# A two-stage convolution and joint network with its gradients: the rows of ge by small transfers and a shuffle, the last chunk on 128 partitions, and some squares allowed on GpSimd

## The chip, the cores and the metric

The kernel runs on one core of one Trainium2 chip. The metric is device time in microseconds (us) of that core. A core has five engines that run their own instruction streams in order: TensorE (PE; its weight loads are PEld), VectorE (DVE), ScalarE (ACT), GpSimd (POOL) and SyncE (SP, which here only issues DMAs). They wait for one another by semaphores. The kernel before was timed in three runs, and one further execution was profiled.

## The reference: what is computed

```python
# B, T, D, K, U = 2, 16000, 256, 3, 8;  T1 = T/2, T2 = T/4
h  = gelu(conv3(x, w1))[:, ::2]            # (B, 8000, 256)
f  = gelu(conv3(h, w2))[:, ::2]            # (B, 4000, 256)
fe = f @ w_f                               # (B, 4000, 256)
ge = g @ w_g                               # (B, 8, 256)
j  = tanh(fe[:, :, None] + ge[:, None])    # (B, 4000, 8, 256)
out = j @ w_o                              # (B, 4000, 8, 256)
# and, for a given grad_out of out's shape, the gradients of x, w1, w2, g, w_f, w_g and w_o
```

The bulk of the work hangs on `j`, which has eight rows (u) for each of the 8000 positions. For each u the kernel computes the tanh, `out`, the product of grad_out with w_o transposed, its product with j squared minus one (whose sums over positions and over u give the gradients of ge and fe), and w_o's gradient, which is j's rows times grad_out.

## The kernel before

**Tiling.** The 8000 positions of both sequences are cut into 17 chunks: one of 256, fifteen of 512 and a last one of 64. A chunk lies in blocks of up to 128 positions (`A` blocks of `Pw`). Chunk 8 holds the end of sequence 0 and the start of sequence 1. Channels lie on the 128 partitions in two halves (kt, mt); this is the transposed layout. Matmuls that sum over positions, as w_o's gradient does, need the other layout, positions on partitions, which the code calls rows.

**Stages.** `stage_a` does both convolutions of a chunk and FE, the projection fe. `stage_j` does everything with eight u, in four pairs (`pair`). `stage_de` goes back through the convolutions and adds up the weight gradients of the chunk. `gg_out` ends with the gradients of g, w_g and w_o. While chunk k is in `stage_j`, chunk k+1 is in `stage_a` and chunk k-1 in `stage_de`.

**One pair of u** (line 634 on): ACT computes JT, the tanh with ge as its bias (L644). JR, the same tanh in rows, comes in one of two ways. In chunks 0 and 1 (`TRANS`) PE transposes JT (L663) and ACT or DVE moves the result out of PSUM. In the other chunks DVE adds FER (fe in rows, made in `stage_a`) and GEB (ge's eight rows, the same on each partition; L668) and ACT takes the tanh (L673). PE adds JR times GO, the loaded grad_out, to the sum GWO; GWO stays in PSUM for the whole kernel. GOT is GO transposed by a DMA. PE multiplies it by w_o transposed (WOT), DVE multiplies the result by JSQ minus one (L716, with the sum over positions as a second output), and the results of the eight u are added up in ZS by DVE (L733), the last into NGFE (L730). JSQ is JT squared, by ACT (L703) or DVE (L705). PE computes JT times w_o in four blocks, ACT or DVE moves them to OUT_SB (L345, L350), and SP stores them.

**GEB** (`make_geb`, line 602): PE multiplies w_g by one column of ge's input repeated over 128 columns, so that the result stands on each partition: 16 matmuls of 256 columns and four moves of 512 out of PSUM. It is made three times: for sequence 0, for sequence 1 and, as GEBX, for chunk 8, where POOL first fills GM with the columns of both (L608).

**The last chunk** has 64 positions in one block, so its blocks of rows fill 64 partitions. Its GO is one load with all eight u, and its GOT one DMA transpose.

**What sets the order.** The code gives each operation an engine (or two that may take it), a cost, a due time and the buffers that it reads and writes. `Flow.issue` (line 107) plays all of it through on these costs before anything runs, and writes the instruction streams in the order in which operations start there. A small edit thus moves operations in every stream. Buffers come from classes with a few slots (`jsq` has 2, `go`, `got` and `out` have 3, `ps`, the PSUM banks, has 7), and an operation that opens a buffer waits until a slot is free. The choice of ACT or DVE for a move, too, is made there.

Most matmuls carry line 336 in the profile (the helper `mm`), moves out of PSUM lines 345 to 352 (`evac`), DMAs lines 360 and 362.

Of the kernel before, what the change touches and what calls it, by code (L numbers as in the profile page):

```python
# [12 lines left out]
ALU = mybir.AluOpType  # L13
# [207 lines left out]
def kernel(  # L221
# [99 lines left out]
    W2T = fixed([P, KT, KK * D], BF16, "W2T")  # L321
    W1T = fixed([P, KT, KK * D], BF16, "W1T")
    GR8 = fixed([U, B, D], BF16, "GR8")
    ACC1 = fixed([P, KK, KT, D], FP32, "ACC1")
# [95 lines left out]
    def load_go(k, up, at, after=()):  # L420
        c = chunks[k]
        A, Pw = c.A, c.Pw
        GO = buf("go", [P, NB, 2, V], BF16, "GO")
        if c.last:

            dma("SP", lambda: GO[:Pw].rearrange("p a u v -> p (a u v)"),
                lambda: bass.AP(tensor=go_.tensor, offset=go_.offset + c.c0 * U * V, ap=[[U * V, Pw], [1, U * V]]),
                r=[], w=[GO], bytes_=Pw * U * V * 2, new=[GO], at=at, after=after)
            st[k]["GO"] = {up: GO for up in range(UP)}
            return  # L430
        dma("SP", lambda: GO[:Pw, 0:A].rearrange("p a u v -> p a (u v)"),
            lambda: bass.AP(tensor=go_.tensor, offset=go_.offset + (c.c0 * U + 2 * up) * V,
                            ap=[[A * U * V, Pw], [U * V, A], [1, 2 * V]]),
            r=[], w=[GO], bytes_=Pw * A * 1024, new=[GO], at=at, after=after, sub="go")
        st[k].setdefault("GO", {})[up] = GO

    def load_got(k, up, at):
        c = chunks[k]
        A, Pw = c.A, c.Pw
        GO = st[k]["GO"][up]  # L440
        GOT = buf("got", [P, NB, 2, KT, P], BF16, "GOT")
        if c.last:
            dma("SP", lambda: GOT[:, :, :, :, :Pw].rearrange("p a u k c -> p (a u k) c"),
                lambda: GO[:Pw].rearrange("p a u v -> p (a u v)"), r=[GO], w=[GOT],
                bytes_=Pw * U * V * 2, new=[GOT], transpose=True, at=at)
            st[k]["GOT"] = {up: GOT for up in range(UP)}
            return
        dma("SP", lambda: GOT[:, 0:A, :, :, :Pw].rearrange("p a u k c -> p (a u k) c"),
            lambda: GO[:Pw, 0:A].rearrange("p a u v -> p (a u v)"), r=[GO], w=[GOT],
            bytes_=Pw * A * 1024, new=[GOT], transpose=True, at=at, sub="got")  # L450
        st[k].setdefault("GOT", {})[up] = GOT
# [86 lines left out]
    def stage_a(k, t0, dt):  # L538
# [45 lines left out]
        for mt in range(KT):  # L584
# [6 lines left out]
            evac(lambda mt=mt: FE[:, 0:A, mt, :Pw], lambda ps=ps: fl(ps[:, :W], A), W, r=[ps], w=[(FE, mt)])  # L591
        if k not in TRANS:
            S["FER"] = rows(k, "fer", "FER", FE, 0, A, [(FE, 0), (FE, 1)], pe=Pw, lag=0.0 if c.first else 500.0)
# [4 lines left out]

    n_gwo = sum(len(c.blk) for c in chunks) * U * KT
    gwo_cnt = [0]  # L600

    def make_geb(kind):
        GEB = buf("gx" if kind == "x" else "geb", [P, U, D], BF16, "GEB")
        if kind == "x":
            px = [c.px for c in chunks if c.px is not None][0]
            GM = buf("out", [P, KT, U, P], BF16, "GM")
            for b, lo, hi in ((0, 0, px), (1, px, P)):
                op("POOL", 1200.0, lambda e, b=b, lo=lo, hi=hi: nc.gpsimd.tensor_copy(  # L608
                    out=GM[:, :, :, lo:hi], in_=gT[b][:].unsqueeze(3).to_broadcast([P, KT, U, hi - lo])),
                   r=[gT[b]], w=[(GM, b)], new=[GM] if b == 0 else [])  # L610
            rd = [GM]
        else:
            rd = [gT[kind]]
        for u2 in range(UP):
            ps = psum()

            def mms(e, u2=u2, ps=ps):
                for j in range(2):
                    u = 2 * u2 + j
                    for kt in range(KT):  # L620
                        lhsT = GM[:, kt, u, :] if kind == "x" else gT[kind][:, kt, u:u + 1].to_broadcast([P, P])
                        mm(ps[:, j * D:(j + 1) * D], lhsT, WG[:, kt, :], kt == 0, kt == KT - 1)
            op("PE", c_pe([D] * 4), mms, r=rd + [WG], w=[ps], new=[ps] + ([GEB] if u2 == 0 else []))
            evac(lambda u2=u2: GEB[:, 2 * u2:2 * u2 + 2].rearrange("p u d -> p (u d)"), lambda ps=ps: ps[:], 512,
                 r=[ps], w=[(GEB, u2)])
        return GEB

    def stage_j(k, t0, dt, GEB):
# [3 lines left out]
        FE = S["FE"]  # L632

        def pair(up):
            F.now = tu = t0 + dt * up / UP
            q = dt / UP
            JT = buf("jt", [P, 2, KT, CW], BF16, "JT")
            GOT, GO = S["GOT"].pop(up), S["GO"].pop(up)
            u0 = up if c.last else 0
            for j in range(2):  # L640
                for mt in range(KT):
                    def jt(e, j=j, mt=mt):
                        for b, lo, hi, _ in c.segs:
                            nc.scalar.activation(  # L644
                                out=fl(JT[:, j, mt, :W], A)[:, :, lo:hi], in_=FE[:, 0:A, mt, lo:hi], func=ACT.Tanh,
                                bias=GE[:, b, mt, 2 * up + j:2 * up + j + 1], scale=1.0)
                    op("ACT", sum(c_act((s[2] - s[1]) * A, ptr=True) for s in c.segs), jt,
                       r=[(FE, mt)] + [(GE, s[0]) for s in c.segs], w=[(JT, (j, mt))],
                       new=[JT] if j == 0 and mt == 0 else [], at=tu - q * (1.0 - (2 * j + mt) / 4), sub="jt")
            halves = [c.blk[h:h + 2] for h in range(0, A, 2)]  # L650
            for h, tbs in enumerate(halves):
                JR = buf("jr", [P, 2, 2, D], BF16, "JR")
                th = tu + q * (h / 2 - 0.5)
                n, lo, m = len(tbs), tbs[0][0], Pw
                if k in TRANS:
                    tr = psum(BF16)
# [19 lines left out]
                def gwo(e, tbs=tbs, JR=JR):  # L676
                    for tb, m in tbs:
                        for j in range(2):
                            for d2 in range(KT):
                                n = gwo_cnt[0]  # L680
                                mm(GWO[:, d2, :], JR[:m, tb % 2, j, d2 * P:(d2 + 1) * P], GO[:m, up if c.last else tb, j, :],
                                   n == 0, n == n_gwo - 1)
                                gwo_cnt[0] = n + 1
                op("PE", c_pe([V] * (4 * n)), gwo, r=[JR, GO], w=[], at=tu + q * (h / 2 + 0.3), sub="gwo")
            OUT = buf("out", [P, NB, 2, V], BF16, "OUT_SB")
            for step in range(4):
# [5 lines left out]
                def gj(e, j=j, d2=d2, ps=ps):  # L692
                    for kt in range(KT):
                        mm(fl(ps[:, :W], A), WOT[:, kt, d2 * P:(d2 + 1) * P], GOT[:, u0:u0 + A, j, kt, :Pw], kt == 0, kt == KT - 1)
                if u and d2 == 0:
                    NGZ = buf("ngz", [P, KT, CW], FP32, "NGZ")
                op("PE", c_pe([W] * KT), gj, r=[GOT, WOT], w=[ps], new=[ps, NGZ] if u and d2 == 0 else [ps])
                if d2 == 0:
                    JSQ = buf("jsq", [P, KT, CW], BF16, "JSQ")

                    def jsq(e, j=j, JSQ=JSQ):
                        if e == "ACT":
                            nc.scalar.activation(out=JSQ[:, :, :W], in_=JT[:, j, :, :W], func=ACT.Square)  # L703
                        else:
                            nc.vector.tensor_tensor(out=JSQ[:, :, :W], in0=JT[:, j, :, :W], in1=JT[:, j, :, :W], op=ALU.mult)  # L705
                    op(("ACT", "DVE"), (c_act(KT * W), c_dve(KT * W, 0.5)), jsq, r=[(JT, (j, 0)), (JT, (j, 1))], w=[JSQ],
                       new=[JSQ], at=F.now - q / 4, sub="jsq")
# [28 lines left out]
                for tb, m in c.blk:  # L736
                    if tb != step:
                        continue
                    ps = psum()

                    def out_mm(e, tb=tb, m=m, ps=ps):
                        for jj in range(2):
                            for kt in range(KT):
# [4 lines left out]
                         r=[ps], w=[(OUT, tb)])  # L748
            F.now = tu + q
            dma("SP", lambda: bass.AP(tensor=o_.tensor, offset=o_.offset + (c.c0 * U + 2 * up) * V,  # L750
                                      ap=[[A * U * V, Pw], [U * V, A], [1, 2 * V]]),
# [24 lines left out]
    def stage_de(k, t0, dt):  # L776
# [136 lines left out]
        for bl, m in c.sblk:  # L913
# [21 lines left out]
            if bl % 2 == 1 or bl == A - 1:  # L935
# [4 lines left out]
                def put(p0, p1, lo, hi, GX=GX, row=row):  # L940
                    dma("SP", lambda: row_ap(gx_, row + 4 * A * p0 + lo, 4 * A, p1 - p0, hi - lo),
                        lambda: GX[p0:p1].rearrange("p a c d -> p (a c d)")[:, lo * D:hi * D], r=[GX], w=[],
# [123 lines left out]
    make_ge()  # L1066
    GEB = make_geb(0)
    GEBX = None
    for k in range(NG + 1):
# [15 lines left out]
        if k + 1 < NG and chunks[k + 1].px is not None:  # L1085
            F.now = t0 + Wk * 0.3
            GEBX = make_geb("x")
        if k < NG:
            F.stage = "j" + part(k)
            stage_j(k, t0, Wk, GEBX if c.px is not None else GEB)  # L1090
        if k < NG and c.px is not None:
            F.now = t0 + Wk * 0.3
            GEB = make_geb(1)
        if k + 1 < NG:
# [42 lines left out]
```

## Time and profile before

| what | us |
|---|---|
| three timed runs | 794.16, 795.49 (median), 795.92 |
| the profiled execution: its time | 793.3 |
| the profiled execution: first to last instruction (span) | 791.0 |
| PE busy in the span | 773.1 (98%) |
| ACT busy | 727.0 (92%) |
| DVE busy | 716.1 (91%) |
| POOL busy | 83.8 (11%) |

The granted TensorE clock was 0.998 over the span. Busy times of PE count a matmul from its start to its modelled end, and neighbours overlap, so two things tell more than the share: the gaps between matmuls, and the spacing of their starts. All four streams can be read as a timeline, as busy time in windows, and as a chain of waits that is followed back from the last instruction.

### The profile page before, as it was taken

The numbers are of one execution on the slowest core, as the hardware profiler recorded it, in microseconds if no ns is written. First come the engines' busy times: TensorE is split into PE (matmuls) and PEld (weight loads), VectorE is DVE, ScalarE is ACT, GpSimd is POOL, SyncE is SP. The second block draws the span as 40 slices with busy tenths as digits, with TensorE's granted clock in tenths as the row PEclk, the third lists the DMA queues.
The fourth block names the chain that finished last, engine by engine and source line by source line (L and its number), as shares of the span: only waits on it lengthen the run. The fifth ranks groups of instructions, "written<-read, shape, count | busy, mean of one in ns | idle before, by whom it ended". The sixth has DMA issues, their size and how long they took to land.

```text
span 791.0 us, 15682 instructions
## 1 busy us (share of the span) xinstructions
PE 773.1 (98%) x5687; PEld 537.9 (68%) x5722; DVE 716.1 (91%) x1514; ACT 727.0 (92%) x1176; POOL 83.8 (11%) x227
## 2 busy tenths in 40 slices
PE   8989999999999999999999999999999999999996
PEld 6657577576675767767677675776767767577764
DVE  5899999897998989999999898989989899899874
ACT  6999999999999998999999998999999999898752
POOL 2110010201002011110101102010020110102010
PEclk9999999999999999999999999999999999999999
DMA  9999999999999899999999999998999999999874
GB/s 208 205 190 202 214 263 229 244 228 281 202 231 256 231 238 195 229 267 219 233 218 254 228 217 233 214 264 209 230 235 214 239 237 228 237 264 255 201 177 123
DMA packets 381809, 178.82 MB, mean 226 GB/s; under 512 B 307586, under 2 KB 375460, under 8 KB 379812
## 3 DMA queue, kind: packets, MB, share of 16 engines
q1 hardware_dynamic: 380516, 177.03, 99.8%
q8 instruction: 45, 0.74, 0.4%
q10 hardware_dynamic: 1056, 0.52, 0.2%
q14 instruction: 32, 0.26, 0.1%
q0 software_dynamic: 160, 0.27, 0.1%
HBM read 51.42 MB, written 50.34 MB: 129 GB/s over the span
## 4 chain that ended last, share of the span: by engine, by line
PE 72%; ACT 11%; DVE 9%; DMA 3%; issue 3%; SPq 1%; POOL 0%; DVEq 0%; ACTq 0%
PE ps L336 60%; PE GWO L336 10%; ACT JT L644 2%; DVE g_s L516 2%; ACT JSQ L703 2%; DMA GOT<-GO 2%; ACT g_sq L510 2%; PE psb L489 2%; DVE NGZ L716 1%; ACT OUT_SB L345 1%; ACT JR L673 1%; DVE g_sq L529 1%; SPq L360 1%; ACT HTo L513 1%; DMA XC<-in_x_dram 1%
## 5 line engine op out<-in xcount | busy, mean ns | idle before, releaser
L644 ACT ACTIVATE JT<-FE,GE 128x512 bf16<-128x512 bf16 (+4 forms) x288 | 180.7, 680 | 0.0
L716 DVE SCALAR_TENSOR_TENSOR NGZ<-JSQ,ps 128x512 f32<-128x512 bf16 (+3 forms) x252 | 149.7, 607 | 2.5 <-PE ps L336 2.0
L336 PE MATMUL ps<-WO,JT 128*128 128x256 bf16 (+1 forms) x1008 | 148.2, 273 | 1.3 <-DVE NGZ L716 1.3
L336 PE MATMUL ps<-GOT,WOT 128*128 128x512 bf16 (+2 forms) x544 | 146.5, 362 | 1.8 <-DMA GOT<-GO 1.6
L345 ACT CAST OUT_SB<-ps 128x512 bf16<-128x512 f32 (+1 forms) x210 | 123.0, 600 | 17.4 <-PE ps L336 17.3
L703 ACT ACTIVATE JSQ<-JT 128x1024 bf16<-128x1024 bf16 (+2 forms) x128 | 128.6, 1005 | 9.2 <-DVE NGZ L716 8.2
L336 PEld LDWEIGHTS <-JT 128*128 128x128 bf16 (+1 forms) x1008 | 98.2, 98 | 54.9 <-issue 2.0
L336 PE MATMUL GWO<-GO,JR 128*128 128x256 bf16 (+1 forms) x1008 | 130.8, 273 | 0.1
L673 ACT ACTIVATE JR<-JR 128x1024 bf16<-128x1024 bf16 (+1 forms) x116 | 121.6, 1054 | 4.1 <-DVE JR L668 3.8
L733 DVE TENSOR_TENSOR ZS<-ZS,NGZ 128x1024 f32<-128x1024 f32 (+2 forms) x102 | 115.1, 1128 | 0.3
L336 PEld LDWEIGHTS <-JR 128*128 128x128 bf16 (+1 forms) x1008 | 98.2, 98 | 17.8 <-issue 1.3
L516 DVE SCALAR_TENSOR_TENSOR g_s<-g_sq,ps 128x512 bf16<-128x512 bf16 (+2 forms) x102 | 65.2, 639 | 41.0 <-ACT HTo L513 32.2
L336 PEld LDWEIGHTS <-W 128*128 128x128 bf16 x612 | 58.1, 98 | 59.5 <-issue 2.2
L336 PE MATMUL ps<-XC,W 128*128 128x512 bf16 (+2 forms) x408 | 84.3, 362 | 0.9 <-DMA XC<-in_x_dram 0.9
L668 DVE TENSOR_TENSOR JR<-FER,GEB 128x1024 bf16<-128x1024 bf16 (+1 forms) x116 | 79.2, 684 | 2.2 <-PE GWO L336 1.0
L336 PEld LDWEIGHTS <-X 128*128 128x128 bf16 (+1 forms) x756 | 73.8, 98 | 9.4
L772 DVE TENSOR_TENSOR ACC<-ACC,ps 128x512 f32<-128x512 f32 x90 | 59.4, 678 | 16.9 <-PE ps L336 16.7
L336 PEld LDWEIGHTS <-WOT 128*128 128x128 bf16 x544 | 51.6, 98 | 23.9 <-DMA GOT<-GO 1.8
L347 ACT ACTIVATE GX_SB<-ps 128x512 bf16<-128x512 f32 (+1 forms) x109 | 64.1, 615 | 1.6 <-PE ps L336 1.1
L510 ACT ACTIVATE g_sq<-ps 128x512 bf16<-128x512 f32 (+2 forms) x102 | 59.1, 580 | 3.4 <-PE ps L336 2.7
L525 ACT ACTIVATE g_s<-g_s 128x1024 bf16<-128x1024 bf16 (+2 forms) x51 | 52.1, 1025 | 6.3 <-DVE g_s L516 6.1
L336 PE MATMUL ps<-GHoR,X 128*128 128x256 bf16 (+1 forms) x378 | 57.7, 273 | 0.0
(139 smaller groups left out, 1113.6 us busy)
## 6 DMA issues: line engine op xcount, KB each, us to landing
GO<-in_grad_out_dram SPq DMA_DIRECT2D x60, 512.0 KB, 5.3
out_dram<-OUT_SB SPq DMA_DIRECT2D x60, 512.0 KB, 5.3
X<-in_x_dram SPq DMA_DIRECT2D x15, 1088.0 KB, 8.3
out_dram<-GX_SB SPq DMA_DIRECT2D x30, 512.0 KB, 5.5
GO<-in_grad_out_dram SPq DMA_DIRECT2D x5, 256.0 KB, 5.4
GOT<-GO SPq DMA_TRANSPOSE x65, 5.0
out_dram<-OUT_SB SPq DMA_DIRECT2D x4, 256.0 KB, 3.5
XC<-in_x_dram SPq DMA_TRANSPOSE x62, 5.5
```

The lines of the kernel that those rows point to most:

```text
L336: nc.tensor.matmul(ps_ap, lhsT=lhsT, rhs=rhs, start=start, stop=stop)
L345: nc.scalar.copy(out=dst(), in_=src())
L347: nc.scalar.activation(out=dst(), in_=src(), func=ACT.Copy, scale=scale)
L510: op("ACT", c_act(W, True), lambda e, mt=mt, ps=ps: nc.scalar.activation(out=sq[:, 0:A, mt, :Pw], in_=fl(ps[:, :W], A), func=ACT.Square, s ...
L516: op("DVE", c_dve(W), lambda e, mt=mt, ps=ps: nc.vector.scalar_tensor_tensor(out=s[:, 0:A, mt, :Pw], in0=sq[:, 0:A, mt, :Pw], scalar=1.0, ...
L644: nc.scalar.activation(out=fl(JT[:, j, mt, :W], A)[:, :, lo:hi], in_=FE[:, 0:A, mt, lo:hi], func=ACT.Tanh, bias=GE[:, b, mt, 2 * up + j:2 ...
L668: op("DVE", c_dve(n * 2 * D, 0.5), lambda e, lo=lo, n=n, m=m, JR=JR: nc.vector.tensor_tensor(out=JR[:m, 0:n], in0=S["FER"][:m, lo:lo + n]. ...
L673: op("ACT", c_act(n * 2 * D), lambda e, n=n, m=m, JR=JR: nc.scalar.activation(out=JR[:m, 0:n], in_=JR[:m, 0:n], func=ACT.Tanh), r=[JR], w= ...
L703: nc.scalar.activation(out=JSQ[:, :, :W], in_=JT[:, j, :, :W], func=ACT.Square)
L716: nc.vector.scalar_tensor_tensor(out=fl(zap(), A)[:, :, lo:hi], in0=fl(JSQ[:, d2, :W], A)[:, :, lo:hi], scalar=1.0, in1=fl(ps[:, :W], A)[: ...
L733: nc.vector.tensor_tensor(out=a, in0=a, in1=b, op=ALU.add)
L772: op("DVE", c_dve(512), lambda e: nc.vector.tensor_tensor(out=acc_ap().rearrange("p k d -> p (k d)"), in0=acc_ap().rearrange("p k d -> p ( ...
```

## The change

Four edits:

1. **GEB.** PE computes ge's rows once for each sequence, 8 partitions by 256, and they are moved to a small tile GER. GEB is set to zero on POOL; four DMAs of 4 KB from POOL's queue write all eight rows into partitions 0, 32, 64 and 96; a VectorE shuffle copies the first partition of each group of 32 to the whole group. GEB of the second sequence is made the same way. GEBX is put together by two DVE copies out of both.
2. **The last chunk.** Two u stand side by side: the odd u of a pair on partitions 64 to 127. GO comes by two loads, GOT by a transpose of 128 partitions, JR by PE transposes of JT, and w_o's gradient and `out` by half as many matmuls. Its four stores of `out` become two, after the last pair. FER of that chunk is not made.
3. **Squares.** In chunks 0 and 1 an operation JSQ may also go to POOL, as a product.
4. **Stores.** The last chunk's stores of x's gradient are issued by ACT and no longer by SP.

The core of the diff:

```diff
+    def make_geb(b):
+        GEB = buf("geb", [P, U, D], BF16, "GEB")
+        op("POOL", 2100.0, lambda e: nc.gpsimd.memset(GEB[:], 0.0), r=[(GER, b)], w=[GEB], new=[GEB])
+        for q in range(0, P, 32):
+            dma("POOL", lambda q=q: GEB[q:q + 1], lambda: GER[:, b, :], r=[(GER, b)], w=[(GEB, q)], bytes_=4096)
+        def spread(e):
+            v = GEB[:].rearrange("p u d -> p (u d)").bitcast(FP32)
+            nc.vector.stream_shuffle(v, v, [0] * 32)
+        op("DVE", 66.0 + c_dve(U * D // 2), spread, r=[GEB], w=[GEB], sub="geb", lag=45000.0 if b == 0 else 100000.0)
+        return GEB
+    def mix_geb(G0, G1):
+        px = [c.px for c in chunks if c.px is not None][0]
+        GEB = buf("gx", [P, U, D], BF16, "GEB")
+        op("DVE", c_dve(U * D, 0.25), lambda e: nc.vector.tensor_copy(out=GEB[:], in_=G1[:]), r=[G1], w=[GEB], new=[GEB])
+        op("DVE", c_dve(U * D, 0.25), lambda e: nc.vector.tensor_copy(out=GEB[:px], in_=G0[:px]), r=[G0], w=[GEB])
+        return GEB
+    def ge_rows():
+        for b in range(B):
+            ps = psum()
+            def mms(e, b=b, ps=ps):
+                for kt in range(KT):
+                    mm(ps[:U, 0:D], gT[b][:, kt, :], WG[:, kt, :], kt == 0, kt == KT - 1)
+            op("PE", c_pe([D] * KT), mms, r=[gT[b], WG], w=[ps], new=[ps])
+            evac(lambda b=b: GER[:, b], lambda ps=ps: ps[:U, 0:D], D, r=[ps], w=[(GER, b)])
...
+                if c.last:
+                    tr = psum(BF16)
+                    def trs(e, tr=tr):
+                        for kt in range(KT):
+                            nc.tensor.transpose(out=tr[:2 * Pw, kt * P:(kt + 1) * P], in_=JT[:, 0, kt, :2 * Pw], identity=ident[:])
...
-                        for j in range(2):
+                        for j in range(1 if c.last else 2):
...
                     def jsq(e, j=j, JSQ=JSQ):
+                        if e == "POOL":
+                            nc.gpsimd.tensor_tensor(out=JSQ[:, :, :W], in0=jtw(JT, j), in1=jtw(JT, j), op=ALU.mult)
...
-                    op(("ACT", "DVE"), (c_act(KT * W), c_dve(KT * W, 0.5)), jsq, r=[(JT, (j, 0)), (JT, (j, 1))], w=[JSQ],
+                    pool = k < 2
+                    op(("ACT", "DVE", "POOL") if pool else ("ACT", "DVE"),
+                       (c_act(KT * W), c_dve(KT * W, 0.5)) + ((100.0 + 2.0 * KT * W,) if pool else ()), jsq, r=[(JT, (j, 0)), (JT, (j, 1))], w=[JSQ],
...
-                    dma("SP", lambda: row_ap(gx_, row + 4 * A * p0 + lo, 4 * A, p1 - p0, hi - lo),
+                    dma("ACT" if c.last else "SP", lambda: row_ap(gx_, row + 4 * A * p0 + lo, 4 * A, p1 - p0, hi - lo),
...
-    GEB = make_geb(0)
-    GEBX = None
+    GEB = GEBX = None
...
         if k + 1 < NG and chunks[k + 1].px is not None:
             F.now = t0 + Wk * 0.3
-            GEBX = make_geb("x")
+            GEB1 = make_geb(1)
+            GEBX = mix_geb(GEB, GEB1)
+        if k == 1:
+            F.now = t0 + Wk * 0.1
+            ge_rows()
+            GEB = make_geb(0)
```

## The prediction, made before the changed kernel had run

> **What bounds the kernel now.** I read the page's first part and the head of the chain of waits first:
>
> ```profile
> PE 773.1 (98%) x5687; PEld 537.9 (68%) x5722; DVE 716.1 (91%) x1514; ACT 727.0 (92%) x1176; POOL 83.8 (11%) x227
> ...
> PE 72%; ACT 11%; DVE 9%; DMA 3%; issue 3%; SPq 1%; POOL 0%; DVEq 0%; ACTq 0%
> ```
>
> Three engines are above 90%, so shares settle little. Busy time in windows of 20 us tells where PE has air (columns: stretch, its length, then busy us and instructions of PE, PEld, DVE, ACT, POOL, then clock, DMA share, GB/s):
>
> ```profile
> 0.00:20.00 20.00, 16.55 (x140) 13.13 (x141) 11.98 (x40) 13.10 (x32) 4.79 (x17) 1.00 0.96 207
> 20.00:40.00 20.00, 19.62 (x149) 13.00 (x148) 17.95 (x45) 19.63 (x36) 2.08 (x7) 1.00 1.15 207
> 40.00:60.00 20.00, 17.30 (x129) 11.33 (x128) 18.41 (x49) 20.00 (x33) 3.66 (x11) 1.00 1.04 187
> 60.00:80.00 20.00, 19.95 (x174) 15.25 (x173) 19.78 (x40) 19.82 (x33) 0.53 (x2) 1.00 1.02 210
> 80.00:100.00 20.00, 18.43 (x123) 11.34 (x122) 18.32 (x37) 18.84 (x30) 1.70 (x7) 1.00 0.94 216
> ...
> 460.00:480.00 20.00, 20.00 (x155) 14.87 (x153) 18.89 (x38) 18.95 (x28) 0.70 (x3) 1.00 1.00 225
> ...
> 760.00:780.00 20.00, 18.70 (x171) 14.10 (x170) 12.39 (x57) 7.60 (x18) 1.62 (x6) 1.00 0.68 175
> ```
>
> From 100 to 720 us PE is full: in the timeline its matmuls start 0.216 us (512 columns) or 0.109 us (256) apart, almost without a gap. There, PE work that goes is time that goes. Only the ramp (0 to 90) and the end leave PE waiting. The chain names what holds the ramp (start, length, what):
>
> ```profile
> 12.08 0.20 DVE g_s L533
> ...
> 14.05 0.89 ACT JT L644 x2
> 14.94 0.47 ACT GEB L345
> ...
> 28.88 0.70 DVE g_s L516
> ...
> 44.93 1.03 PE ps L336 x8
> ...
> 75.88 5.20 DMA GO<-in_grad_out_dram
> ...
> 81.15 8.07 DMA GOT<-GO
> ```
>
> ACT holds the time from 13.5 to 28.9, DVE from there to 44.9, PE to 76; then a load of GO and its transpose end late, and PE stands from 87.4 to 89.3.
>
> **The sum, against the profiled execution** (span 791.0, its time 793.3; the median of the timed runs is 795.49, so I add the change to that). Counts are from the order of the built changed program, which has no times.
>
> *PE work.* Out go 48 matmuls of GEB and GEBX (48 x 0.109 = 5.23 us) and, in the last chunk, 8 of GWO and 8 of `out` (1.74). In come four for GER (0.44) and six more transposes (six by 0.057, from L663's spacing, 0.34). Net 6.2 us less. By place: 3.05 in the ramp, as both GEB stand at 13.3 to 16.4 and 22.8; 1.74 for GEBX, near 340; 1.40 in the last chunk. The last two lie where PE is full: **-3.15**.
>
> *Ramp.* Less PE work does not help here; ACT and DVE set the pace. I follow the second chunk's NGFE, which DVE writes at 86.9 and PE takes at 90.1.
> - ACT from its first JT to the second chunk's HTo: the order has two GEB moves fewer (0.47 each, by their spacing), one JR move fewer (0.90), one square fewer (0.53) and one OUT_SB move more (0.47): **-1.9**. DVE loses 2.9 us before the first NGFE (its instructions there, each at the median spacing of its kind, add up to 31.4 and not 34.3), but waits for ACT in that stretch, so I give nothing for it. From the first NGFE to the second it is 39.3 and 39.2.
> - GEB's two memsets on POOL stand in the order right behind G1o's (11.75 us) with no wait. From rows of L368 (512 elements 0.52, 1280 elements 1.16 us) one takes 1.8 us. DVE's L533 at 12.08 is on the chain, and such copies and scalings do not pass a POOL instruction: at 728.11 an L531 took 0.26 instead of 0.19 us under a memset that ended at 728.32. So L533 ends some **+1.6** later (0 if it does pass).
> - The squares. Eight go to POOL: two of 512 elements (chunk 0) and six of 1024 (chunk 1). [...]
>
> ```profile
> 309.89 2.21 POOL L608 COPY GM<-gT 128x640 bf16<-128x640 bf16 x2 [9.21 <-DMA out_dram<-OUT_SB]
> ```
>
> ```profile
> 310.80 1.58 DVE L533 TENSOR_SCALAR g_s<-g_s 128x1024 bf16<-128x1024 bf16 x1
> ```
>
> This L533 usually takes 0.42; it ended only after the second copy (310.54, 1.56 us long). L668 with two SBUF operands took 0.86 at 240.27 instead of 0.68, against a POOL copy of 0.39. Instructions that read PSUM (L716, L350) never stretched. The price of a square: no row has a POOL product. POOL's copies (254 elements 0.39, 1408 elements 1.56) give about 1.2 us for 1024 elements of one operand and 2.3 for two read one after the other; I take 2.1, nearer the second, and half for 512. What DVE loses by it lies between nothing and all of it. In the order, an instruction that can be shut out is followed by one or two that read PSUM, 0.6 each, so some 1.3 pass beside a square: **0.8** lost for each large one, 0.3 for a small one. Ahead of the first NGFE stand the two small ones and one large: +1.4. Behind it stand five: 4.0, less the 2.4 us that DVE idles between both NGFE (41.75 us for 39.3 of work): **+1.6**.
> - The GOT wait at 87.4 lies behind these delays: **-1.7**.
>
> Sum of the ramp: -1.9 + 1.6 + 1.4 + 1.6 - 1.7 = **+1.0**.
>
> [...]
>
> *End.* In the order 10.7 us of PE work stand behind the last chunk's NGFE, where there were 5.5; PE's gap of 1.25 at 777.2, which waits for it, is filled: **-1.0**. SP's last two stores are a stage at 787.24, which landed at 789.67, and 1 x 768 of GX at 787.80. With GX on ACT, the stage moves up one issue (0.57) and is the last: **-0.7**.
>
> *At nothing.* The DMAs of GEB are issued by POOL at about 17 to 25 us, at 0.61 each like GR's, and the shuffle is needed at some 85, where L668 starts; without that cover all of DVE would stand behind it. Shuffle and GEBX's copies add some 2 x 1.15 (as L733's 1.2 for 1024 words; 0.4 as L527 at the least) and 2 x 0.65 us to DVE, which has more than 1 us of air in each window where PE is full, and loses seven GEB moves. The last chunk's two loads of GO and its transpose have some 6 us until PE reads GOT at 762.2; smaller rows of 512 B could eat that. ACT and DVE wait for PE from 746 on, so fewer moves there give nothing.
>
> Total: -3.15 + 1.0 - 1.7 = **-3.8**: span 787.2, this execution 789.5, and for the median **791.7**.
>
> **Rivals.**
> - *The squares are free* (chance 0.27). DVE reads PSUM while POOL works, and the memsets pass. For it: twenty L733 that overlapped POOL never stretched (at most 1.22 us); it was POOL that waited (G1o's copy at 154.13 took 1.33 us, not 0.39). Then the ramp gives -1.9 - 1.7, the total -8.5: **787.0**.
> - *The squares shut DVE out nearly whole* (0.16), the slower end. Each large one costs 1.8, each small one 0.6: 3.0 ahead of the first NGFE, 9.0 - 2.4 behind it; ramp -1.9 + 1.6 + 3.0 + 6.6 - 1.7 = +7.6, total +2.7: **798.2**. It decides from 1.4 us a large square on (0.8 + 3.8 / 6). For it: five large squares come in the 42 us where DVE idles 2.4; against it: POOL has to wait too. [...]
> - *The change does not do what it says* (0.14): PE is let go, but the new order waits elsewhere by as much, as with GEBX's copies in front of DVE's moves in chunk 7, or GO's two loads: **795.5**, no change.
> - The forecast, -6 to -1.7, has 0.43.
>
> **Numbers.** A change under 0.2% (1.6 us) can hardly be told from none. Faster: 0.43 and 0.27, less 0.02 for the edge: 0.68; same 0.15; slower 0.17. Range 786.0 to 797.5: the free squares with 1 us below them, and above it most of the shut-out case is left. The bounds reach further (a full 2.1 for each square and no gain at the end: some 804), with little chance.
>
> **What would show it.** PE's matmuls fewer by 54 and its idle time from 100 to 720 unchanged; in the windows 20 to 100, DVE instructions with two SBUF operands stretched to 1 us and more beside POOL products of about 2.1; L533 of chunk 0 late by 1.6 behind a memset; the second NGFE 2.7 us behind the 86.9, and no wait for GOT after it; no gap of PE at the last NGFE. Wrong it is if the products take under 1.3 us, if DVE's ramp is not longer, or if PE shows new gaps in the middle.

## The result, and the profile after

The changed kernel took 797.81 us (median of 7 runs, 796.86 to 798.32), the kernel before, on the same chip, 794.16 (7 runs, 792.32 to 795.92): a ratio of **1.0046**, 95% interval 1.0027 to 1.0064. It is slower by some 3.7 us, where 3.8 us less had been forecast. The profiled execution took 798.25, its span is 796.5 (791.0 before).

In the changed kernel the lines of the code have moved: L533, the scaling that the prediction names, is L537; L529 is L533, L527 is L531; the product of a square is L726; L716 (the product with JSQ) is L743, L733 (the sum in ZS) is L760, L668 (FER plus GEB) is L686. The first part of its page and the head of its chain of waits:

```profile
PE 774.9 (97%) x5668; PEld 535.5 (67%) x5668; DVE 720.5 (90%) x1500; ACT 723.1 (91%) x1173; POOL 108.4 (14%) x243
...
PE 85%; DVE 7%; ACT 5%; issue 2%; DMA 1%; DVEq 0%; ACTq 0%
```

POOL has 24.6 us more, DVE 4.4 us more although it has fewer instructions, and PE's share fell. Busy time in windows of 20 us says where (columns as before: PE, PEld, DVE, ACT, POOL, then the granted clock):

```profile
0.00:20.00 20.00, 13.20 (x82) 8.86 (x82) 10.37 (x27) 8.14 (x21) 8.24 (x19) 0.93 0.88 192
20.00:40.00 20.00, 19.00 (x140) 13.29 (x141) 14.61 (x43) 17.75 (x35) 7.18 (x16) 0.90 0.85 177
40.00:60.00 20.00, 17.77 (x103) 9.53 (x102) 19.66 (x41) 16.76 (x28) 7.79 (x9) 0.91 1.09 209
60.00:80.00 20.00, 17.13 (x145) 12.51 (x144) 20.00 (x38) 16.66 (x28) 7.27 (x10) 1.00 0.64 151
80.00:100.00 20.00, 19.12 (x169) 15.04 (x167) 19.97 (x37) 16.79 (x29) 4.78 (x2) 1.00 0.96 200
...
460.00:480.00 20.00, 19.45 (x146) 13.63 (x144) 20.00 (x42) 19.95 (x31) 0.00 (x0) 1.00 1.00 211
```

Three things are to be seen. From 60 to 80 PE lacks 2.9 us where it lacked nothing, while DVE is busy without a pause: DVE paces the ramp. In the first window PE does 58 matmuls fewer, of which only 28 are GEB's, which edit 1 takes away, and ACT is busy for 8.1 us instead of 13.1: something held all engines early. And the granted clock, 1.00 in each of these windows before, is 0.90 to 0.93 in the first three. Behind 100 us PE is as full as it was. The second chunk's NGFE, which the prediction followed, is written at 99.49 us (86.89 before), and from where PE takes it to the end it is 696.3 us (700.9): the loss is all ahead of it, and the gain behind it is there.

**The memsets.** POOL's and DVE's timelines of the changed kernel at 13 us (start, length, what):

```profile
13.20 0.39 POOL L379 COPY G1o<-G1o 128x254 bf16<-128x254 bf16 x1 [3.12 <-DVE G1o L539]
13.54 0.10 POOL L369 MEMSET G1o<- 128x2 bf16 x1
13.57 3.54 POOL L609 MEMSET GEB<- 128x2048 bf16 x2
```

```profile
13.38 0.50 DVE L533 TENSOR_TENSOR g_sq<-g_sq,HTe 128x512 bf16<-128x512 bf16 x1
13.79 3.46 DVE L537 TENSOR_SCALAR g_s<-g_s 128x512 bf16<-128x512 bf16 x1
17.18 0.27 DVE L535 TENSOR_SCALAR g_sq<-g_sq 128x512 bf16<-128x512 bf16 x1
```

Both memsets run back to back, 1.80 us each, and L537, which takes 0.29 us elsewhere, ends only after the second: 3.2 us, on the chain ("13.87 3.38 DVE g_s L537" stands in it).

**The squares.** The same two views where DVE is without a pause:

```profile
57.48 1.89 POOL L726 TENSOR_TENSOR JSQ<-JT 128x1024 bf16<-128x1024 bf16 x1
...
63.01 1.89 POOL L726 TENSOR_TENSOR JSQ<-JT 128x1024 bf16<-128x1024 bf16 x1 [0.79 <-ACT JR L346]
...
71.49 2.19 POOL L726 TENSOR_TENSOR JSQ<-JT 128x1024 bf16<-128x1024 bf16 x1 [0.32 <-DVE NGZ L743]
```

```profile
57.97 1.69 DVE L531 TENSOR_SCALAR g_sq<-g_sq 128x1024 bf16<-128x1024 bf16 x1
...
62.78 0.68 DVE L520 SCALAR_TENSOR_TENSOR g_s<-g_sq,ps 128x512 bf16<-128x512 bf16 x1
63.38 2.60 DVE L760 TENSOR_TENSOR ZS<-ZS,NGZ 128x1024 f32<-128x1024 f32 x1
...
71.93 0.69 DVE L520 SCALAR_TENSOR_TENSOR g_s<-g_sq,ps 128x512 bf16<-128x512 bf16 x1
72.53 2.23 DVE L760 TENSOR_TENSOR ZS<-ZS,NGZ 128x1024 f32<-128x1024 f32 x1
```

L531 takes 0.43 us elsewhere, L760 1.22. Each of these ends about its own usual time after the product's end (63.01 + 1.89 = 64.90; 64.90 + 1.22 = 66.12, and L760 ends at 65.98): it started beside the product and ended as late as if it had run only behind it. L520, which takes an operand from PSUM, keeps its 0.68 beside the product. I call the time that an instruction takes above the median of its kind its stretch. Over the ramp the stretches beside the eight products add up to 8.4 us: 0.83 beside the small ones, 1.69, 1.26, 1.39, 1.01, 1.70 and 0.49 beside the six large.

**The rest.** The wait for GOT at 87 us is gone. The shuffle took 1.30 us and waited for nothing. PE's work, from the number and columns of its matmuls, is 6.2 us less, as counted. At the end, though, PE still waits for the last NGFE:

```profile
777.94 0.34 PE L337 MATMUL ps<-GOT,WOT 128*128 128x64 bf16 x6
779.44 0.38 PE L337 MATMUL ps<-NGFE,WFT 128*128 128x64 bf16 x4 [1.16 <-DVE NGFE L757]
```

### The profile page after: what moved, and what is told of

The parts are those of the page before. It is cut to its first block, busy times and chain, and to the rows that moved or that the text cites. A ratio compares the mean times of both kernels' runs of the same rounds, so it can differ in the third digit from the quotient of the medians.

```text
span 796.5 us, 15651 instructions
## 1 busy us (share of the span) xinstructions
PE 774.9 (97%) x5668; PEld 535.5 (67%) x5668; DVE 720.5 (90%) x1500; ACT 723.1 (91%) x1173; POOL 108.4 (14%) x243
## 4 chain that ended last, share of the span: by engine, by line
PE 85%; DVE 7%; ACT 5%; issue 2%; DMA 1%; DVEq 0%; ACTq 0%
PE ps L337 71%; PE GWO L337 12%; DVE g_s L520 2%; PE psb L493 2%; DVE NGZ L743 1%; ACT JT L654 1%; ACT OUT_SB L346 1%; DMA XC<-in_x_dram 1%; DVE g_sq L533 1%; ACT JR L691 1%; DVE ZS L760 1%; DVE g_sq L531 1%; DVE g_s L537 1%; ACT g_sq L514 1%; ACT JSQ L728 1%
## 5 line engine op out<-in xcount | busy, mean ns | idle before, releaser
L743 DVE SCALAR_TENSOR_TENSOR NGZ<-JSQ,ps 128x512 f32<-128x512 bf16 (+3 forms) x252 | 149.8, 607 | 4.1 <-PE ps L337 3.6
L337 PE MATMUL ps<-WO,JT 128*128 128x256 bf16 x1000 | 150.1, 274 | 0.0
L337 PEld LDWEIGHTS <-JT 128*128 128x128 bf16 x1000 | 98.0, 98 | 55.7 <-issue 0.8
L337 PE MATMUL GWO<-GO,JR 128*128 128x256 bf16 x1000 | 130.0, 273 | 0.8 <-ACT JR L691 0.5
L691 ACT ACTIVATE JR<-JR 128x1024 bf16<-128x1024 bf16 x112 | 119.0, 1066 | 9.8 <-DVE JR L686 9.7
L760 DVE TENSOR_TENSOR ZS<-ZS,NGZ 128x1024 f32<-128x1024 f32 (+2 forms) x102 | 121.8, 1194 | 0.4
L337 PEld LDWEIGHTS <-JR 128*128 128x128 bf16 x1000 | 97.7, 98 | 16.4 <-ACT JR L691 1.0
L520 DVE SCALAR_TENSOR_TENSOR g_s<-g_sq,ps 128x512 bf16<-128x512 bf16 (+2 forms) x102 | 65.0, 639 | 41.1 <-ACT HTo L517 32.3
L337 PE MATMUL ps<-XC,W 128*128 128x512 bf16 (+2 forms) x408 | 87.6, 371 | 1.3 <-DMA XC<-in_x_dram 0.9
L686 DVE TENSOR_TENSOR JR<-FER,GEB 128x1024 bf16<-128x1024 bf16 x112 | 78.1, 702 | 1.1 <-PE GWO L337 0.9
L379 POOL COPY GF<-GF 128x254 bf16<-128x254 bf16 (+1 forms) x17 | 7.0, 412 | 453.4 <-issue 315.1
L337 PE MATMUL ps<-W1T,GHo 128*128 128x512 bf16 (+1 forms) x252 | 61.3, 326 | 0.0
```

The costliest lines, as they stand in the source:

```text
L337: nc.tensor.matmul(ps_ap, lhsT=lhsT, rhs=rhs, start=start, stop=stop)
L520: op("DVE", c_dve(W), lambda e, mt=mt, ps=ps: nc.vector.scalar_tensor_tensor(out=s[:, 0:A, mt, :Pw], in0=sq[:, 0:A, mt, :Pw], scalar=1.0, ...
L686: op("DVE", c_dve(n * 2 * D, 0.5), lambda e, lo=lo, n=n, m=m, JR=JR: nc.vector.tensor_tensor(out=JR[:m, 0:n], in0=S["FER"][:m, lo:lo + n]. ...
L691: op("ACT", c_act(n * 2 * D), lambda e, n=n, m=m, JR=JR: nc.scalar.activation(out=JR[:m, 0:n], in_=JR[:m, 0:n], func=ACT.Tanh), r=[JR], w= ...
L743: nc.vector.scalar_tensor_tensor(out=fl(zap(), A)[:, :, lo:hi], in0=fl(JSQ[:, d2, :W], A)[:, :, lo:hi], scalar=1.0, in1=fl(ps[:, :W], A)[: ...
L760: nc.vector.tensor_tensor(out=a, in0=a, in1=b, op=ALU.add)
```

## The experiments

Theories: **M**, the memsets hold the ramp; **S**, the squares take DVE's time; **C**, PE's idle time lowers its clock, and that costs; **A**, ACT and DVE are both short of time, and what one gains the other gives back. Later came **P**: the squares cost only where PE is not late itself. All medians stand beside the kernel before on the same chip, whose medians lay between 793.9 and 794.6. A median of these kernels moves by about 1 us from one group of runs to the next, and by more where a group has only five or six runs: those of e5 lie between 785.5 and 789.6.

### First: each suspect taken out of the changed kernel

**e1**, GEB's zeros by DVE at the start:

```diff
+    GEBF = [fixed([P, U, D], BF16, f"GEBF{b}") for b in range(B)]
...
-        GEB = buf("geb", [P, U, D], BF16, "GEB")
-        op("POOL", 2100.0, lambda e: nc.gpsimd.memset(GEB[:], 0.0), r=[(GER, b)], w=[GEB], new=[GEB])
+        GEB = GEBF[b]
+        op("POOL", 2100.0, lambda e: None, r=[(GER, b)], w=[GEB])
...
     def warm_up(e):
...
+        [nc.vector.memset(g[:], 0.0) for g in GEBF]
```

> The changed kernel with one thing taken away: both GEB tiles have places of their own and are set to zero by DVE at the very start, so POOL's two memsets (13.57 to 17.11 us, 1.80 us each) are gone; all streams are otherwise in the same order. Theory M (the memsets shut out chunk 0's L537 for 3.2 us, and ACT's first JT, which came at 19.0 instead of 14.1, with it): L537 takes 0.29 us again, the first JT comes at some 15.8, and the run is 3 us shorter than the changed kernel: about 794.6. Rival S (the squares on POOL alone set the ramp; DVE has the 3 us back from later waits): 797 to 798, and the second NGFE still near 99.5.

Measured 791.4 (ratio 0.9971, 0.9959 to 0.9983). L537 takes 0.28, ACT's first JT comes at 15.9 and not at 19.0. Theory M holds, but the gain is 6.4 us and not 3.2. Another 1.2 of it is seen: with all moved by 3 us, L760 no longer falls on the product that stretched it by 1.70 at 85.3; an L539 is stretched by 0.48 there. That makes 4.4 us, and the two profiled executions differ by 4.8 (798.25 and 793.5). The profiled execution was the longest of e1's twelve (790.5 to 793.5); why the others are up to 3 us shorter isn't shown.

**e2**, no square on POOL, and **e3**, a constant written in the place of the squares:

```diff
-                    pool = k < 2
+                    pool = False
```

```diff
-                            nc.gpsimd.tensor_tensor(out=JSQ[:, :, :W], in0=jtw(JT, j), in1=jtw(JT, j), op=ALU.mult)
+                            nc.gpsimd.memset(JSQ[:, :, :W], 0.25)
```

> The changed kernel with no square allowed on POOL: the eight go back to ACT or DVE, as the planner chooses, and it moves other operations of the ramp with them. Theory S (POOL's products shut out DVE instructions with two SBUF operands, some 8.4 us in the ramp): no L760, L531 or L686 stretched by over 0.3 us from 30 us on, the second NGFE 5 to 8 us sooner than 99.5, time 790 to 793. Rival A (ACT is as short of time in the ramp as DVE, and takes back by the squares what DVE gains): the stretches go, but the NGFE stays within 2 us of 99.5 and the time within 796 to 799.

> The changed kernel in which POOL writes a constant into the eight JSQ of chunks 0 and 1 and does not square (it leaves the eight squares out); the streams are in the same order. POOL's instruction then reads nothing and writes the same 1024 elements; by the memset of 2048 elements in 1.80 us it takes some 0.9 us (estimate). Theory S in the form that any POOL instruction shuts DVE out while it lasts: stretches of DVE beside them of 0.4 to 0.9 us each, their sum near 4 instead of 8.4, time 793 to 795. In the form that it is POOL's reading of two operands that shuts DVE out: no stretches, 790 to 791. Rival A (not DVE's stretches but ACT's and PE's order sets the ramp): 797 to 798.

e2: 790.55 (0.9964, 0.995 to 0.9978), 7.3 us less than the change; NGFE at 92.9. e3: 789.63 (0.9956, 0.9939 to 0.9973), 8.2 less; NGFE at 90.6. Theory S holds and A falls: the squares given back to ACT and DVE cost no more than the 0.9 us between these two. In e3's timelines POOL and DVE stand side by side as in the change:

```profile
53.35 0.95 POOL L726 MEMSET JSQ<- 128x1024 bf16 x1
...
57.84 0.95 POOL L726 MEMSET JSQ<- 128x1024 bf16 x1 [0.70 <-DVE NGZ L743]
```

```profile
53.87 0.72 DVE L531 TENSOR_SCALAR g_sq<-g_sq 128x1024 bf16<-128x1024 bf16 x1
...
58.30 1.22 DVE L760 TENSOR_TENSOR ZS<-ZS,NGZ 128x1024 f32<-128x1024 f32 x1
```

L760 starts inside POOL's memset and keeps its 1.22; only L531, as L537 in the ramp, waits for a memset (0.72 for 0.43). So the sum of two SBUF tiles was held up beside a product, which reads SBUF (2.60), and not beside a memset, which only writes it (1.22); the scalings, with one SBUF operand, were held up by a product (L531, 1.69 for 0.43) and by memsets (L531, 0.72; L537, 3.46 for 0.29 beside two). With the order unchanged, removing 8.1 of the 8.4 us of stretches gave 8.2 us: one for one. A memset is also shorter than a product (0.95 and 1.89 us), so JSQ is ready sooner; but in neither trace does DVE wait for POOL's JSQ in the ramp. Nor is it the granted clock: e3's executions had 0.991 to 0.996, those of the change 0.993 to 0.995.

**e4**, idle matmuls in the place where GEB's had stood:

```diff
+                if b == 1:
+                    for _ in range(24):
+                        mm(GWO[:, 0, :], WG[:, 0, 0:P], WG[:, 0, :], True, True)
```

> The changed kernel with 24 matmuls of 256 columns of no use put on PE right behind the matmuls that make GE (15.0 us), where PE otherwise stands idle until 17.8 and where the kernel before had its 28 matmuls of GEB; no other stream changes. Theory C (PE's idle time there is why the granted clock fell to 0.5 from 17.12 to 23.95, and that holds the path): the clock stays at 1.0 there, GE's rows and chunk 0's transposes come sooner, and the run is 1 to 2 us shorter: 796. Rival: PE waits for ACT and DVE in that stretch and the half clock costs nothing: 797.5 to 798.5. A third: the fall of the clock has another cause than the idle time and stays, 798.

Measured 796.81 (1.0038, 1.0023 to 1.0054). The clock did stay up. Windows of e4 and, for the changed kernel, those above:

```profile
0.00:20.00 20.00, 14.46 (x120) 10.95 (x121) 12.06 (x32) 10.00 (x25) 8.62 (x20) 1.00 1.01 204
20.00:40.00 20.00, 19.01 (x149) 13.26 (x147) 15.69 (x42) 18.64 (x36) 8.55 (x17) 1.00 1.06 193
40.00:60.00 20.00, 16.34 (x113) 9.60 (x112) 19.65 (x45) 16.93 (x27) 7.31 (x11) 1.00 0.94 195
```

In the changed kernel all seven executions had a mean clock of 0.993 to 0.995; with the idle matmuls all eight had 0.997 to 1.000. So with PE's idle time at 15 us filled the clock stayed up (1.00 in the three windows, 0.90 to 0.93 without), as C says; but the 1.0 us is no more than the two intervals leave open. What the half clock costs here may be anything from nothing to some 2.5 us, an estimate from these intervals.

### Second: both cures, and the parts alone

**e5** joins e1's and e2's edits; **e10** adds e4's.

> The changed kernel with both cures: GEB's zeros by DVE at the start and no square on POOL. Theories M and S together (memsets 3.2 us, squares some 4 to 7, each on the path): 797.8 - 3.2 - 4 to 7 = 787.6 to 790.6 by stretches alone, and 784.2 if the two gains measured one at a time (6.4 and 7.2) add up. The stretches of DVE beside POOL up to 110 us add up to under 0.6 us. Rival A (with the squares back, ACT or DVE is the bound of the ramp, and the memsets are hidden behind it): no better than no squares on POOL alone, 790 to 791.

> Both cures, and the 24 idle matmuls behind GE's. Theory C (idle PE lowers the granted clock in the ramp, and that costs up to 1.3 us in an execution in which it does): 1 us less than both cures alone, with a granted clock of 0.997 or more in nearly every execution and a smaller spread. Rival (the clock falls anyway at other places, or PE waits for ACT and DVE there): within 0.5 us of both cures alone.

e5: **787.41** (0.9919, 0.9902 to 0.9937), faster than both kernels. PE's window from 60 to 80 is full again:

```profile
60.00:80.00 20.00, 20.00 (x162) 14.14 (x159) 20.00 (x42) 20.00 (x34) 2.02 (x5) 1.00 0.96 188
```

Measured from e5, the memsets cost 3.1 us (790.55), as M says, and the squares 4.0 (791.4). e10: 787.61; the idle matmuls bring nothing, C's price is not seen in these medians. Yet among e5's six executions the two with the lowest mean clock, 0.993, are the longest (789.2 and 789.6), and the one with 0.999 is the shortest (785.5). Whether the clock made them longer, no run tests.

**e6**, the kernel before with the last chunk's edits and the stores alone, and **e7**, with the squares alone. e6 is the changed kernel with edit 1 taken back and e2's line; e7 is the kernel before with

```diff
+                        if e == "POOL":
+                            nc.gpsimd.tensor_tensor(out=JSQ[:, :, :W], in0=JT[:, j, :, :W], in1=JT[:, j, :, :W], op=ALU.mult)
...
+                    pool = k < 2
```

> The kernel before with the edits of the last chunk and of its stores alone (GEB as before, no square on POOL). By the prediction's terms (1.4 us of PE work in the last chunk, the gap of 1.0 at the last NGFE, 0.7 of the stores): 794.1 - 3.1 = 791.0, with the ramp unchanged and its second NGFE at 86.9. Rival: the end waits for its loads and stores and not for PE's work, 793 to 794.

> The kernel before with the squares of chunks 0 and 1 allowed on POOL and nothing else: the planner puts four of 512 elements and four of 1024 there. Theory S (a large one takes 1.3 us of DVE, a small one 0.8, of which DVE's idle time absorbs 1.4): 4 x 1.3 + 4 x 0.8 - 1.4 = 7, less the 1.7 of the wait for GOT that lies behind the delay: 794.1 + 5 = 799. Rival: before's ramp, with PE busier and no memsets, has slack enough for DVE, and the squares relieve ACT: 793 to 796.

e6: 789.89 (0.9951, 0.9934 to 0.9968), a gain of 4.2. PE's idle time from 740 us on fell by 1.5 (6.75 to 5.28), and its work, by count, by 1.4. e7: 793.83 (1.0002, 0.9992 to 1.0012): **no change**, though the instructions beside its four small and four large products are stretched by some 6 us. This went against S, and the next runs were made for it.

### Third: why squares alone cost nothing

**e8**, edit 1 alone; **e9**, the change without edit 1; **e11**, e6 with GEBX by DVE's copies and both GEB by PE. e9 differs from the change by

```diff
-            GEB1 = make_geb(1)
-            GEBX = mix_geb(GEB, GEB1)
+            GEBX = make_geb("x")
...
-            ge_rows()
-            GEB = make_geb(0)
```

with the old `make_geb`, called where it was; e8 is the reverse, put into the kernel before; e11 adds to e6

```diff
-            GEBX = make_geb("x")
+            GEB1 = make_geb(1)
+            GEBX = mix_geb(GEB, GEB1)
```

> The kernel before with the edit of GEB alone. The two memsets come with it, and PE's work of 4.8 us goes, 1.74 of it (GEBX) where PE is full. Theory M with C (the memsets hold the ramp for 3.2 us, and the idle time that the removed matmuls leave on PE lowers the granted clock for some 1.3 us more; the 3.05 us of PE work that goes in the ramp gives nothing): 794.1 - 1.7 + 3.2 + 1.3 = 797. Rival (the memsets alone hold it): 795.5. Second rival (all 4.8 us of PE's work count, less the memsets): 792.5.

> The changed kernel with the edit of GEB undone: last chunk, stores and squares on POOL (four of 512 elements, four of 1024). It differs by the squares alone from the run with the last chunk's edits only (789.9). Theory P (the squares' stretches of DVE cost nothing as long as PE, with GEB's matmuls in the ramp, is late itself, as the run with the squares alone showed by 793.8 against 794.1): 789.5 to 790.5. Theory S (they cost what DVE loses, and the wait for GOT hid it in that run): 791.5 to 794.

> The last chunk's edits and its stores, both GEB by PE in the ramp as before, and of the edit of GEB only that GEBX is put together by two DVE copies: no memset, no square on POOL. If PE's work in the ramp is free and that near 340 us is not: 789.9 - 1.7 = 788.2, with no half clock ahead of 40 us. If all of PE's work counts, the run with both cures (787.4), which has 3.05 us less of it in the ramp, stays 2 to 3 us faster than this one. If DVE's copies stand in front of PE's buffers in chunk 7: no gain, 790.

e8: 793.48 (0.9988, 0.9972 to 1.0004), between the forecasts of 792.5 and 795.5 and not 797: the memsets are in it, and edit 1 still does not lose. e9: 790.79 (0.9945, 0.9924 to 0.9967), 0.9 above e6: as e7, squares for almost nothing. e11: 794.48 (0.9995, 0.9978 to 1.0011): a miss, 6 us worse than expected from an edit that takes 1.7 us of PE work away. Its trace says where: PE takes the last NGFE at 775.4 us, as in e6 (775.3), but after a gap of 2.0 us, and the end comes 19.4 us later and not 11.2. `Flow.issue` had moved single operations in the last third of PE's stream and rewritten its last tenth, and put 5.9 us more of PE's work behind that NGFE. In the profiled execution (796.55, 2.1 above the median) the clock was halved besides, from 774.69 to 781.52: behind that NGFE stand 112 matmuls, of the same tiles and sizes as in the changed kernel, and PE, busy in 14.73 of 14.75 us, needs 14.75 us for them where the changed kernel needs 11.91 at full clock. Two kernels that differ by one edit differ by the planner's order too.

**e12**, the change with e1's and e4's edits, tests P. **e13** and **e14** are e5 with `pool = k == 0` (two small squares) and `pool = k == 1` (six large).

> The changed kernel with GEB's zeros by DVE at the start, squares on POOL as in the change, and the 24 idle matmuls in the place where GEB's stood. Theory P (the squares cost because PE, without GEB's matmuls, is early and waits for DVE; with 2.6 us of work put back it is late again): within 1 us of the same without squares on POOL, 787.6 to 788.6. Theory S (these squares cost DVE's stretches, whatever PE does at 15 us): 790.5 to 792, as with early zeros alone (791.4).

> Both cures, but the two squares of 512 elements of chunk 0 on POOL. By the stretch measured beside them (0.83 us beside the second, none beside the first): 787.4 + 0.8 = 788.2 where DVE paces the ramp; 787.4 where that is hidden.

> Both cures, but the six squares of 1024 elements of chunk 1 on POOL. If the price of the squares (4.0 us with the memsets cured) is that of the large ones by number and place: 790.5 to 791, with stretches of some 6.5 us of which DVE's and PE's slack takes half. If the small ones and the shift that they bring carry it: 788 to 789.

e12: 791.47 (0.9977, 0.9966 to 0.9988), 3.9 above the same without squares (e10). P falls in this form: with 2.6 us of work put back on PE the squares cost what they did. e13: 790.22 (0.9945, 0.9927 to 0.9964), 2.8 above e5 where 0.8 at most was expected; with 787.2 to 790.4 among its runs, and 785.5 to 789.6 among e5's, 0.8 us can't be told. e14: 793.1 (0.9983, 0.9971 to 0.9994), 5.7 above e5 for 7.5 us of stretches: the large ones carry the price. The small and the large ones apart thus come to 8.5, where all eight together cost 4.0 (e1 against e5): these medians are no finer than some 2 us, and each kernel has an order of its own in the ramp.

**e15** separates the two: e7 with the constant written in place of the squares (e3's edit), all streams in e7's order.

> The kernel before with the squares of chunks 0 and 1 allowed on POOL, in which POOL writes a constant into these eight JSQ and does not square (it leaves the eight squares out): every stream in the same order as in the run with the squares alone. If the stretches of DVE cost there too, and the new order of PE's stream gave them back: 2 to 4 us below 793.8, so 790 to 792. If PE was late anyway and hid them: 793.3 to 794.1.

Measured 788.94 (0.9934, 0.9921 to 0.9946), **4.9 us below e7**. The profiled executions differ by 5.5, and the stretched instructions of e7, each against the same instruction of e15, by 6.2. One of them in e7, where L706 is the product and L740 the sum in ZS, and then in e15:

```profile
43.67 1.92 POOL L706 TENSOR_TENSOR JSQ<-JT 128x1024 bf16<-128x1024 bf16 x1 [2.33 <-DVE NGZ L723]
43.77 2.37 DVE L740 TENSOR_TENSOR ZS<-ZS,NGZ 128x512 f32<-128x512 f32 x1
```

```profile
43.00 1.11 POOL L706 MEMSET JSQ<- 128x1024 bf16 x1 [2.09 <-DVE NGZ L723]
43.14 0.68 DVE L740 TENSOR_TENSOR ZS<-ZS,NGZ 128x512 f32<-128x512 f32 x1
```

Windows of e7 and then of e15 from 40 to 60:

```profile
40.00:60.00 20.00, 16.23 (x100) 9.83 (x98) 19.15 (x38) 15.37 (x27) 9.95 (x12) 0.83 0.88 159
```

```profile
40.00:60.00 20.00, 18.49 (x140) 12.15 (x138) 19.50 (x50) 20.00 (x34) 6.98 (x17) 1.00 1.09 203
```

PE does 40 matmuls more in e15's window; part of that is the clock, 0.83 there in e7. At one mean clock, 0.995, the gap remains: 789.3 and 789.6 in e15, 793.7 to 795.4 in e7. So the squares cost there too most of what DVE loses. What made e7 even is what came with them: told that POOL takes the squares, the planner moved PE's matmuls at many places in the first half of the stream, and ACT and DVE have eight squares less. Without the products' price that is 5.7 us faster than the kernel before (788.94 against 794.62 on the same chip). How much of it is the order and how much the work taken off ACT and DVE, no run separates. In the changed kernel, with edit 1, the same permission moves only PE's first fifth, and brings 0.9 (e2 to e3).

## Why the prediction was wrong, point by point

The runs make a chain from the kernel before to the change; its steps add up by construction, and each is uncertain by 1 to 2 us:

| step | from, to | us |
|---|---|---|
| last chunk and stores | 794.1, 789.9 (e6) | -4.2 |
| GEB by DMAs and shuffle, without the memsets | 789.9, 787.4 (e5) | -2.5 |
| the two memsets | 787.4, 790.55 (e2) | +3.1 |
| squares off ACT and DVE, POOL only writing | 790.55, 789.6 (e3) | -0.9 |
| POOL squaring | 789.6, 797.8 | **+8.2** |

- **The step that failed is the price of the squares**, "0.8 lost for each large one, 0.3 for a small one", 1.4 ahead of the first NGFE and 1.6 behind it: 3.0 in all, where the runs give 8.2. That a product holds up DVE instructions beside it was right, and its length too (2.1 taken, 1.89 measured). Two sizes were wrong. "Some 1.3 pass beside a square" because instructions that read PSUM follow: in fact the shut-out instruction starts 0.1 to 1.0 us after the product in five cases of six, so that a large one cost 1.26 on average; the small ones cost none and 0.83. And "less the 2.4 us that DVE idles between both NGFE" was taken off; with the memsets there, nothing was. (With the memsets cured, 4.0 was lost, or 4.9 without the 0.9 between e2 and e3, for 7.1 us of stretches; there some was.)
- The timeline suggests why they meet, though no run tested it. A product needs a JSQ buffer, of which there are two; the L743 that reads one last frees it, and L760 stands right behind the L743s on DVE. The product at 71.49 had waited for L743 (its note above), and L760 came at 72.53. But only three of the eight have this note; those at 49.95, 63.01 and 85.23, for example, had waited for ACT.
- **The memsets** were placed rightly, but one was counted where two run back to back: 3.2 for L537, 3.1 in the median (e2 against e5), not 1.6.
- **The GOT wait** went as foretold, and the work where PE is full (-3.15) is gone: the stretch from the second NGFE to the end is 4.6 us shorter. That ACT's 1.9 us came back in the ramp isn't shown; e5's gain by edit 1 is 2.5, of which GEBX is 1.74.
- **The end**: the gap that was to be filled, 1.25 in the prediction and 1.09 in the timeline before, is still 1.16. The step took more work behind NGFE for a filling; but PE stood idle for the 1.16 us, and the X products, which stand behind the matmuls of NGFE in its stream, began only after these (779.98 and 779.44). Only work ahead of the NGFE could have filled that wait. The stores gave 0.55 (PE's last matmul to the end: 5.67 before, 5.12), not 0.7. In e6's order the gap was filled, which is part of its 4.2.
- **The clock** was in no term. It fell in each execution of the change (means of 0.993 to 0.995), and what that cost stays open: e4 is only 1.0 below the change, and its interval leaves room for more. At e11's end, where PE was busy in 14.73 of 14.75 us, the half clock cost 2.8 us.
- The rival "the squares shut DVE out nearly whole" (798.2) has the way and nearly the time, but that it is so near is luck. It was to decide from 1.4 us a large square on, and a large one lost 1.26. Its squares came to 9.6 in all (3.0 + 9.0 - 2.4); they cost 8.2, and that much only because no idle time of DVE was left to take off. The second memset (1.5) and the gap that stayed (1.0) make up for the difference. As a change it says +2.7, where +3.7 was measured: the time is nearer because it was counted from 795.49, and the kernel before took 794.16. It had 0.16, because "POOL has to wait too" was held against it. POOL did wait where DVE came first: the last product (91.99) took 2.87 us and not 1.89 behind an L760 (91.88), and the L686 beside its end lost only 0.49. Five of six times POOL came first.

## What to carry to other kernels

Work given to GpSimd was not off VectorE's path here: beside its products, which read SBUF, VectorE's sums of two SBUF operands and a scaling with one lost up to 1.70 of a product's 1.9 us, 1.26 on average. Idle time of VectorE is no safe deduction: the run lost 8.2 us for 8.4 of stretches in the change, and 4 to 5 for 6 to 7 in two other cases. Zeros for a buffer were better written where nothing on the path runs, at the very start, than on GpSimd beside work on the path: the two memsets held one scaling up by 3.2 us, and the run without them (e1) was 6.4 us shorter. Where a planner writes the order, an edit's price and the new order's price are two things; the same order with the suspected operation made harmless (a write in place of a read) separates the operation's price from the rest, and a comparison of two planned kernels does not.

## What the runs showed of the hardware

In the profiled execution of the changed kernel the granted clock was halved from 17.12 to 23.95 us and from 51.25 to 54.67. Ahead of the first stretch PE stood idle from 13.1 to 14.3 and from 15.2 to 17.8; in the 6.85 us ahead of the second it was busy for 4.74, and its longest gap was 0.70. In e5 the clock was halved for 3.41 us at 46.0. How much idle time lowers the clock, no run shows.

When the clock first rose also varied. Behind the same 20 matmuls from 1.06 us on, its first record of full speed stands at 5.59 us before and at 10.29 in the change, and the first 12 matmuls of XC took 2.72 us there and not 1.47. This alone makes that piece 1.25 us longer, and it is no part of the edit.
